# Block attention with a gated product: transposing q, k and the probabilities in two halves of 64 rows

## The chip, the core and the metric

The kernel runs on one core of a Trainium2 chip. The metric is the device time of one execution in microseconds (us), as the median of several executions. TensorE (PE in the rows) multiplies; its weight loads are listed apart as PEld. VectorE is DVE, ScalarE is ACT, GpSimd is POOL, and SyncE (SP) issues the DMAs.

## The reference

Attention over four batches of 8 heads, 768 positions and 64 columns a head, and a two-layer product over its result:

```python
k_sum = k.reshape(B, H, nb, 32, D).max(axis=3)        # 24 block maxima a head
v_sum = v.reshape(B, H, nb, 32, D).mean(axis=3)
scores_l = where(|i - j| < 16, scale * q @ k.T, -1e9)  # a window of 31 keys
scores_s = scale * q @ k_sum.T + log(32)
a = softmax(concatenate([scores_l, scores_s]))         # + 1e-9 in the divisor
x = a @ concatenate([v, v_sum])                        # then heads side by side: 3072 x 512
h = x @ w_in                                           # 512 -> 2048
out = (h - tanh(h)) @ w_out                            # 2048 -> 512
```

All inputs and the output are float32.

## The kernel before

**Tiling.** The 3072 positions are cut into 8 units (u) of 384, two to a batch, and a unit into three tiles of 128 rows. A unit has four pairs (p) of heads, so there are 32 pairs in all. The 16 column groups (f) of the 2048-wide layer run 22 slots behind the attention (LAG), so that from about 45 us on the two products of an earlier unit and the attention of a later one share TensorE. Products go in two parts, a rounded high word and a rest, three matmuls for one; units 2 to 7 combine two units at a time with seven products in place of eight.

**One pair.** `prep` (L821) transposes q and, from unit 2 on, the four tiles of keys of the pair, so that head columns lie on partitions: a transpose is a TensorE matmul of a 128x128 block against the identity. It is one task, "turn": three blocks of q into PSUM bank pS1 and four of k into bank pX. Two copies bring them to SBUF: "q high" (384 columns) and "k high" (512 columns). In unit 1 only q is transposed there, since the keys of units 0 and 1 are transposed once, in unit 0. `score` (L890) multiplies in blocks of 64x64, four of them side by side in the array, into banks pS0 and pS1. `softmax` (L923) leaves the probabilities of three tiles, each 128 rows x 118 columns for each of two heads. `transpose_probs` (L960) transposes a tile's two blocks in a task "p turn" and copies the 256 columns to SBUF in a task "p out"; the main loop calls it for the tiles one by one, with banks pS0, pX, pS1 (L1344). Then `value` (L900) multiplies them with v in blocks 64 columns wide, two side by side, into bank pX; the value matmuls of a pair stand in one task with the score matmuls of the next pair.

**Order.** The tasks are not emitted in the order of the code. `Plan.schedule` (L167) starts from costs a task, runs a list scheduler over the five engines, and emits the instructions in the order that it finds; on every engine they then run in that order, each waiting on semaphores for what it needs. Among ready tasks the one with the highest `level` goes first. The level is the longest chain of costs to the end, plus numbers from two tables: BIAS by task and KB by kind and phase. A third table (SL) says when a task goes to its second or third engine. A task on TensorE may leave a delay to the next product (LEAVES, L120); scores, values and the small transposes of sums are named there, "turn" and "p turn" are not. Where PE would idle in the first 100 us, matmuls of the identity fill in (`keep_warm`).

All instructions are recorded by a helper, so their line in the profile is L76; the tile names tell them apart. pS is pS0 or pS1, pX the third attention bank, pH the first product, pY0 to pY2 the second. In the profile a plain float32 matmul appears as two instructions, so `value` and `score` show 24 for 12 matmuls; a transpose shows as one.

Of the kernel before, what the change touches and what calls it, by code (L numbers as in the profile page):

```python
# [10 lines left out]
F32 = mybir.dt.float32  # L11
# [24 lines left out]
PROBS, PROBT = 3, 3  # L36
# [7 lines left out]

TOPS = {j: [(0, n)] for n, j in enumerate(PREP)}
SUMS = {1: [(0, 0), (0, 1)], 9: [(0, 2), (0, 3)]}

# [4 lines left out]
KB = {('chunk load', 0): 434.7, ('chunk max', 0): 88.2, ('chunk max', 1): -2.7, ('chunk sum', 0): -220.5, ('chunk sum', 1): -359.7, ('const', 0): -85, ('const', 1): -136.2, ('const', 2): -292.2, ('exp', 0): -33.6, ('g', 0): 13.2, ('g high', 0): -241.1, ('g low', 0): -310.4, ('in first', 0): -71.1, ('in first', 1): -182.2, ('inverse', 0): 28.8, ('join', 0): -293.9, ('join', 1): -75.7, ('k first', 0): -518.8, ('k first', 1): 106.5, ('k first', 2): 448.9, ('k high', 0): -153.3, ('k high', 1): -35.8, ('k keep', 0): 101, ('k keep', 1): -596.6, ('k keep', 2): -249.5, ('k load', 1): -310.2, ('k load', 2): -1.6, ('k move', 0): 111.7, ('k move', 1): -80.4, ('k move', 2): -200.1, ('key turn', 0): -255.8, ('key turn', 1): 120.7, ('key turn', 2): -1.5, ('mean out', 0): -253.8, ('mean out', 1): -79.7, ('mean put', 0): 93.1, ('mean put', 1): -73.6, ('mean put', 2): -2.8, ('mean turn', 1): 1.3, ('mean turn', 2): 20.1, ('min', 0): -0.6, ('normal', 0): 1.9, ('out first', 0): -357.5, ('out first', 1): -259.5, ('p out', 0): -27.4, ('p turn', 0): -1, ('part', 0): 89.2, ('part', 1): 385.1, ('q high', 0): -508.8, ('q load', 0): -35.5, ('q load', 1): 1.5, ('s high', 0): -41.2, ('s high', 1): 1.8, ('s high', 2): -462.5, ('s load', 0): -243.6, ('s load', 1): 1.6, ('s low', 0): 24.9, ('s low', 2): 102.6, ('s mix', 0): -358.8, ('s mix', 2): -480, ('s store', 0): -187, ('s store', 1): 0.7, ('s store', 2): -123.9, ('s whole', 0): 102.7, ('s whole', 1): -1.9, ('s whole', 2): 130.5, ('scores', 0): 1.4, ('seen', 0): 90.1, ('seen', 1): -77, ('seen', 2): -428.9, ('seen max', 0): -210.6, ('seen max', 1): 358.7, ('seen max', 2): 451.2, ('seen turn', 0): -0.7, ('seen turn', 1): 422.3, ('seen turn', 2): -9.1, ('series', 0): -201.9, ('square', 0): -65.5, ('sum', 0): 2.4, ('sum', 1): 419.6, ('sum', 2): -916.3, ('sum guard', 0): 59.1, ('tanh', 0): -2.1, ('top high', 0): 522.9, ('top high', 1): -162.7, ('top max', 0): 10.2, ('top max', 1): 238.5, ('top max', 2): -133.8, ('top pre', 0): -43.1, ('top pre', 1): 183.6, ('top pre', 2): -330.8, ('top put', 0): 0.1, ('top put', 1): -866.6, ('top put', 2): -26.1, ('top turn', 1): -172.1, ('top turn', 2): -472.6, ('turn', 0): 50.1, ('turn', 1): 211.7, ('v load', 1): -28.3, ('values', 1): -139.4, ('w high part 2', 0): -476.2, ('w high part 2', 1): 18.5, ('w high part 2', 2): -45.7, ('w load', 2): 227.6, ('w low', 2): 254.3, ('w low part 2', 0): -652.5, ('w low part 2', 1): -319, ('w low part 2', 2): -478.7, ('w scale', 2): -271.5, ('w shift', 1): 10.3, ('w shift', 2): -314.7, ('w sign', 0): -86.7, ('w sign', 2): -126.7, ('x high', 0): 646, ('x high', 1): -12, ('x low', 0): 282.9, ('x low', 2): -2, ('x mix', 0): 644.6, ('x mix', 1): 18, ('x whole', 0): -1.1, ('x whole', 1): -240.3, ('y out', 0): 157.1, ('y store', 0): -402.7}

HALF = {'const': (12, 12), 'k load': (33, 52), 'q load': (12, 24), 'top pre': (16, 16), 'v load': (44, 82), 'top turn': (8, 8), 'top max': (8, 8), 'q turn': (6, 15), 'q high': (12, 30), 'k turn': (6, 15), 'k high': (6, 15), 'top put': (7, 15), 'scores': (6, 14), 'sum': (8, 8), 'min': (30, 84), 'exp': (30, 84), 'sum out': (8, 8), 'sum guard': (5, 26), 'inverse': (5, 26), 'normal': (30, 84), 'p turn': (15, 42), 'p out': (15, 41), 'mean turn': (2, 4), 'mean out': (2, 4), 'mean put': (6, 14), 'values': (4, 4), 'x whole': (4, 9), 'w load': (13, 32), 'w scale': (12, 32), 'w shift': (12, 32), 'w low': (11, 32), 'w sign': (11, 32), 'w high part 2': (11, 32), 'w low part 2': (7, 32), 'in': (5, 33), 'square': (5, 33), 'tanh': (5, 32), 'series': (5, 32), 'g': (4, 32), 's store': (5, 48), 'out': (7, 96), 'x high': (0, 10), 'x low': (0, 10), 'y out': (0, 6), 'y store': (0, 6), 'g high': (0, 16), 'g low': (0, 16), 's whole': (0, 16), 's mix': (0, 32), 's high': (0, 16), 's low': (0, 16), 'chunk load': (0, 10), 'chunk max': (0, 4), 'chunk sum': (0, 4), 's load': (0, 3), 'x mix': (0, 1), 'top high': (0, 0), 'part': (0, 0), 'join': (0, 0), 'seen': (0, 0), 'seen turn': (0, 0), 'seen max': (0, 0), 'w high part': (3, 26), 'w low part': (3, 26), 'w sign 1': (4, 12), 'w sign 2': (4, 12), 'top low': (1, 2), 'cube': (2, 18), 'big': (2, 17), 'direct': (2, 17), 'pick': (2, 17), 'q low': (0, 2), 'q again': (0, 2), 'k low': (0, 2), 'k again': (0, 2)}


# [254 lines left out]
def program(  # L311
# [509 lines left out]
    def prep(u, p, tags):  # L821
# [4 lines left out]
        def transposes(ps, raw, n):  # L826
# [5 lines left out]
            for i in range(n):  # L832
                tensor.transpose(at(ps)[:, P * i:P * (i + 1)], raw[:, i, hs].rearrange("p a d -> p (a d)"), ident)
# [583 lines left out]
```

## Time and profile before

| What | Value |
|---|---|
| runs of the program | median 685.99 us (685.26 to 686.47, 3 runs) |
| span of the profiled execution | 682.6 us; no other time of this execution is given, and the median of the runs lies 3.4 us above the span |
| PE busy | 659.1 us, 97%, 4885 instructions |
| ACT busy | 491.2 us, 72% |
| DVE busy | 417.4 us, 61% |
| POOL busy | 206.8 us, 30% |
| granted clock of TensorE | 0.996 of full speed |
| DMA | 121.05 MB, 59.6% of 16 engines |

Busy time of PE counts an instruction from its start to its modelled end; matmuls overlap, so the mean of one (ns) is longer than the distance between two starts. How much of PE a kind of instruction takes is therefore read from the starts in the timeline. The number after a bar in the groups is the idle time of that engine before such instructions, with what ended it.

### The profile page before, as it was taken

The numbers are of one execution on the slowest core, as the hardware profiler recorded it, in microseconds if no ns is written. First come the engines' busy times: TensorE is split into PE (matmuls) and PEld (weight loads), VectorE is DVE, ScalarE is ACT, GpSimd is POOL, SyncE is SP. The second block draws the span as 40 slices with busy tenths as digits, with TensorE's granted clock in tenths as the row PEclk, the third lists the DMA queues.
The fourth block names the chain that finished last, engine by engine and source line by source line (L and its number), as shares of the span: only waits on it lengthen the run. The fifth ranks groups of instructions, "written<-read, shape, count | busy, mean of one in ns | idle before, by whom it ended". The sixth has DMA issues, their size and how long they took to land.

```text
span 682.6 us, 14370 instructions
## 1 busy us (share of the span) xinstructions
PE 659.1 (97%) x4885; PEld 549.1 (80%) x4885; DVE 417.4 (61%) x1183; ACT 491.2 (72%) x1445; POOL 206.8 (30%) x336
## 2 busy tenths in 40 slices
PE   7899999899999989999999999999999999999995
PEld 6665555478888877999888889899889889999884
DVE  3889988868897476555584574445576443323551
ACT  4888576778787787768984786766679946555882
POOL 2012222325355545312375642321124110000230
PEclk9999999999999998999999999999999999999999
DMA  8899999853766864785576456758435214453101
GB/s 242 218 260 286 292 291 271 275 156 136 214 190 192 269 186 135 192 220 172 133 233 187 119 139 211 221 156 213 141 116 158 105 62 147 161 170 123 48 1 52
DMA packets 145151, 121.05 MB, mean 177 GB/s; under 512 B 85036, under 2 KB 110892, under 8 KB 145068
## 3 DMA queue, kind: packets, MB, share of 16 engines
q1 hardware_dynamic: 145068, 120.03, 59.6%
q8 instruction: 41, 0.67, 0.4%
q14 instruction: 42, 0.34, 0.2%
HBM read 94.57 MB, written 23.07 MB: 172 GB/s over the span
## 4 chain that ended last, share of the span: by engine, by line
PE 85%; DMA 7%; DVE 3%; ACT 1%; SPq 1%; issue 1%; POOL 1%; ACTq 0%; POOLq 0%; DVEq 0%
PE pY L76 37%; PE pH L76 36%; PE pS L76 7%; PE pX L76 5%; DMA tmp<-in_k_dram 2%; SPq L76 1%; DMA wraw<-in_moe_w_in_dram 1%; DMA gu<-in_v_dram 1%; DMA wh<-in_k_dram 1%; DVE kacc L76 1%; DVE wraw L76 1%; DMA vw<-mean 1%; DMA rawk<-in_k_dram 1%; DMA out_dram<-tmp 1%; DMA scr<-wraw 1%
## 5 line engine op out<-in xcount | busy, mean ns | idle before, releaser
L76 PE MATMUL pY<-wf,gh 128*128 128x512 f32 x432 | 178.1, 439 | 2.9 <-POOL gh L76 2.9
L76 PE MATMUL pH<-wh,wraw 128*128 128x384 f32 x672 | 175.5, 342 | 0.1
L76 PE MATMUL pY<-wh,gh 128*128 128x512 f32 x336 | 137.0, 408 | 0.0
L76 PE MATMUL pY<-wh,gl 128*128 128x512 f32 x336 | 132.7, 395 | 0.0
L76 PEld LDWEIGHTS pH<-wh,wraw 128*128 128x128 f32 x672 | 121.4, 189 | 8.8 <-issue 1.2
L76 PE MATMUL pH<-wf,wraw 128*128 128x384 f32 x309 | 104.2, 337 | 0.0
L76 ACT ACTIVATE prob<-prob,stat 128x118 f32<-128x118 f32 x247 | 92.5, 384 | 12.7 <-DVE stat L76 11.3
L76 PEld LDWEIGHTS pY<-wf,gh 128*128 128x128 f32 x432 | 80.2, 189 | 25.4 <-issue 10.6
L76 PEld LDWEIGHTS pY<-wh,gl 128*128 128x128 f32 x336 | 63.2, 188 | 13.8
L76 POOL TENSOR_TENSOR gu<-gu,gt 128x384 f32<-128x384 f32 x31 | 33.7, 1087 | 128.8 <-ACT gu L76 127.7
L76 PEld LDWEIGHTS pY<-wh,gh 128*128 128x128 f32 x336 | 63.3, 188 | 10.9 <-issue 1.7
L76 ACT ACTIVATE gu<-gu 128x384 f32<-128x384 f32 x128 | 66.6, 521 | 1.8
L76 PE MATMUL pH<-o,wf 128*128 128x384 f32 x188 | 65.1, 442 | 2.0 <-ACT o L76 1.7
L76 PEld LDWEIGHTS pH<-wf,wraw 128*128 128x128 f32 x309 | 58.1, 188 | 0.0
L76 ACT ACTIVATE gu<-pH 128x384 f32<-128x384 f32 x65 | 31.7, 488 | 36.5 <-PE pH L76 33.5
L76 DVE CUSTOM_DVE_ANT_0 prob<-pS,mask 128x118 f32<-128x118 f32 x180 | 40.1, 275 | 28.8 <-PE pS L76 28.8
L76 PEld LDWEIGHTS pH<-o,wf 128*128 128x128 f32 x188 | 34.8, 189 | 19.7 <-issue 2.9
L76 ACT ACTIVATE gv<-pH 128x384 f32<-128x384 f32 x60 | 29.0, 484 | 27.0 <-PE pH L76 26.8
L76 DVE TENSOR_TENSOR gl<-gu,gh 128x384 fp32r<-128x384 f32 x43 | 27.0, 628 | 32.6 <-ACT gh L76 31.8
L76 POOL COPY k<-th 64x72 f32<-64x72 f32 (+1 forms) x45 | 12.7, 282 | 107.9 <-PE pS L76 86.3
L76 DVE TENSOR_TENSOR gu<-gu,gt 128x384 f32<-128x384 f32 x39 | 23.3, 596 | 35.9 <-ACT gu L76 35.8
L76 POOL TENSOR_TENSOR gl<-gu,gh 128x384 fp32r<-128x384 f32 x27 | 29.2, 1081 | 50.8 <-ACT gh L76 28.9
(211 smaller groups left out, 1242.5 us busy)
## 6 DMA issues: line engine op xcount, KB each, us to landing
wraw<-scr SPq DMA_DIRECT2D x75, 512.0 KB
wraw<-in_moe_w_in_dram SPq DMA_DIRECT2D x16, 512.0 KB
wraw<-in_moe_w_out_dram SPq DMA_DIRECT2D x16, 512.0 KB
scr<-wraw SPq DMA_DIRECT2D x16, 512.0 KB
rawq<-in_q_dram SPq DMA_DIRECT2D x42, 128.0 KB
out_dram<-tmp SPq DMA_DIRECT2D x21, 256.0 KB
wraw<-scr SPq DMA_DIRECT2D x21, 256.0 KB
scr<-wh SPq DMA_DIRECT2D x16, 256.0 KB
```

The costliest lines, as they stand in the source:

```text
L76: return lambda *args, **kwargs: self._tc.keep_in_program_order(op(*args, **kwargs))
```

## The change

In units 1 to 7 every 128-row block is transposed as two blocks of 64 rows: rows 0 to 63 with one half of the array's rows into one bank, rows 64 to 127 with the other half into a second bank. A half has the same 128 (or 118) columns as weights, and 64 columns of identity stream through instead of 128. q and k go into pS1 and pX together, half by half; the copies are split by halves too: two of 192 columns for q, two of 256 for k. The probabilities of a pair go, all three tiles, into pS0 and pX, and two copies of 384 columns replace three of 256. A tile's "p turn" is still a task of its own, but both copies wait for all three. Unit 0 keeps its old form. The order is planned anew: the level of a task is now minus a number from one table (TURNS_AT, 66 kinds, 3715 numbers) and no longer holds a chain of costs, BIAS or KB; SL and HALF are other numbers.

```diff
-PROBS, PROBT = 3, 3
+PROBS = 3
+TURN = 0.07
...
-BIAS = {('const', 0): -83.6, ('const', 1): -193.5, ('const', 2): -92.9, ...
+TURNS_AT = {'const': [199.57, 216.39, 42.37, 211.24, 201.89, 329.78, ...
...
-            t.level = max([n.level + (lag if data else 0.0) for n, data in t.next], default=0.0) + BIAS.get(t.name, 0.0) + KB.get((t.kind, phase(t)), 0.0)
+        for t in tasks:
+            at = TURNS_AT.get(t.kind, [0.0])
+            t.level = -at[min(t.name[1], len(at) - 1)]
...
+    def turn_half(out, x, half):
+        rows = slice(64 * half, 64 * half + 64)
+        tensor.transpose(out, x[rows], ident[rows, rows])
...
+        n = NT + 4 if u > 1 else NT
+        def turns():
             for i in range(n):
-                tensor.transpose(at(ps)[:, P * i:P * (i + 1)], raw[:, i, hs].rearrange("p a d -> p (a d)"), ident)
+                for half in range(2):
+                    x = rawq[:, i, hs] if i < NT else rawk[:, i - NT, hs]
+                    turn_half(at(ps[half])[:, 64 * i:64 * i + 64], x.rearrange("p a d -> p (a d)"), half)
+        do("turn", PE, TURN * n, turns, r=[*RAWQ, *(RAWK if u > 1 else []), IDENT], w=[(x, 0) for x in ps])
...
+        for half in range(2):
+            t = ps[half]
+            either("q high", {ACT: 0.28, DVE: 0.29}, lambda e, t=t, half=half: copy(e, at(qf)[:, 0].rearrange("p (i f r) -> p i f r", i=NT, f=2)[:, :, half], ...
+            if u > 1:
+                either("k high", {ACT: 0.32, DVE: 0.36}, lambda e, t=t, half=half: copy(e, k_runs(half), ...
...
+    def turn_probs(u, p, tags):
+        ps = [bank(("t", u, p, half), tag) for half, tag in enumerate(tags)]
+        pt = buf(("pt", u, p), "probT", [P, NT, 2, 2, 64])
+        def go(i):
+            for a in range(2):
+                for half in range(2):
+                    c = 64 * (2 * i + a)
+                    turn_half(at(ps[half])[:N2, c:c + 64], at(("pr", u, p, i))[:, a], half)
+        for i in range(NT):
+            do("p turn", PE, 2 * TURN, lambda i=i: go(i), r=[...], w=[(t, i) for t in ps])
+        for half, t in enumerate(ps):
+            either("p out", {ACT: 0.4, DVE: 0.47}, ..., r=[(t, i) for i in range(NT)], w=[(pt, half)])
...
-            for i, tag in enumerate((tags[2], tags[0], tags[1]) if early else (tags[0], tags[2], tags[1])):
-                transpose_probs(u, p, (i,), (tag,))
+            if early:
+                for i, tag in enumerate((tags[2], tags[0], tags[1])):
+                    transpose_probs(u, p, (i,), (tag,))
+            else:
+                turn_probs(u, p, (tags[0], tags[2]))
```

Three places in the order show it. The first is PE in unit 5. Before, between two pairs there stands (pS_4709 is bank pS0, pS_68 is pS1, rows with `wraw` or `gh` and `gl` are products of an earlier unit):

```order
L76 MATMUL pS_4709<-ident,prob 118x128 x2
L76 MATMUL pS_68<-ident,rawq 128x128 x3
L76 MATMUL pX<-ident,rawk 128x128 x4
L76 MATMUL pH<-q_3027,wraw 128x384 x3
L76 MATMUL pH<-wh_3277,wraw 128x384 x2
L76 MATMUL pH<-wf_3284,wraw 128x384
L76 MATMUL pH<-wh_3444,wraw 128x384 x2
L76 MATMUL pH<-wf_3460,wraw 128x384
L76 MATMUL pH<-wh_3624,wraw 128x384 x2
L76 MATMUL pH<-wf_3642,wraw 128x384
L76 MATMUL pX<-ident,prob 118x128 x2
L76 MATMUL pS_68<-ident,prob 118x128 x2
```

The transposes stand between products in two places, with the full array throughout. In the changed kernel, on PE between the same two pairs, two of the three tiles of probabilities (pS_4934 is pS0) stand together between products:

```order
L76 MATMUL pY_4774<-wh_978,gl 128x512
L76 MATMUL pS_4934<-ident,prob 118x64
L76 MATMUL pX<-ident,prob 118x64
L76 MATMUL pS_4934<-ident,prob 118x64
L76 MATMUL pX<-ident,prob 118x64
L76 MATMUL pS_4934<-ident,prob 118x64
L76 MATMUL pX<-ident,prob 118x64
L76 MATMUL pS_4934<-ident,prob 118x64
L76 MATMUL pX<-ident,prob 118x64
L76 MATMUL pH<-q_3073,wraw 128x384 x3
```

The halves alternate between the two banks, and the third tile comes some forty rows later, alone, after a transpose of block maxima (kacc):

```order
L76 MATMUL pS_68<-ident,kacc 128x96
L76 MATMUL pS_4934<-ident,prob 118x64
L76 MATMUL pX<-ident,prob 118x64
L76 MATMUL pS_4934<-ident,prob 118x64
L76 MATMUL pX<-ident,prob 118x64
L76 MATMUL pY_4863<-wh_1068,gh 128x512
```

So one pair has two stretches of halves for its probabilities, and a third for q and k, each with products ahead and behind it. The second place is PE at the end of unit 3. The changed kernel has this ahead of the values of the unit's last pair (pS_3676 is pS0; vacc is a sum of v, transposed by four small matmuls):

```order
L76 MATMUL pY_3268<-wh_814,gl 128x512
L76 MATMUL pS_3676<-ident,prob 118x64
L76 MATMUL pX<-ident,prob 118x64
L76 MATMUL pS_3676<-ident,prob 118x64
L76 MATMUL pX<-ident,prob 118x64
L76 MATMUL pS_68<-vacc,ident 24x64 x4
L76 MATMUL pX<-probT,vw 64x64 x12
```

Between the last half and the values that read its copy there is only the transpose of a sum. The third place is ACT: the copies of q and k of the changed kernel (q_164, k_82 are their SBUF tiles), between the exponentials and normalisations of a pair:

```order
L76 ACTIVATE prob,stat<-prob,stat 128x118 x3
L76 ACTIVATE q_164<-pX 128x3x64
L76 ACTIVATE q_164<-pS_68 128x3x64
L76 ACTIVATE k_82<-pX 128x4x64
L76 ACTIVATE prob<-prob,stat 128x118
L76 ACTIVATE k_82<-pS_68 128x4x64
```

Four copies stand where two did, each with half the columns.

## Rows read from the trace of the kernel before

**Rows 1.** The page: span, busy time of two engines, the chain by engine

```profile
span 682.6 us, 14370 instructions
...
PE 659.1 (97%) x4885; PEld 549.1 (80%) x4885; DVE 417.4 (61%) x1183; ACT 491.2 (72%) x1445; POOL 206.8 (30%) x336
...
PE 85%; DMA 7%; DVE 3%; ACT 1%; SPq 1%; issue 1%; POOL 1%; ACTq 0%; POOLq 0%; DVEq 0%
```

**Rows 2.** Waits of PE: us in total, times, longest; first and last of 14

```profile
PE pS L76 <- POOL ident L76: 4.3, 1, 4.3
...
PE pY L76 <- ACT probT L76: 0.2, 1, 0.2
```

**Rows 3.** Groups of PE by form: busy us, mean ns of one | idle before

```profile
L76 PE MATMUL pS<-ident,prob 128*118 128x128 f32 x120 | 21.3, 276 | 0.0
L76 PE MATMUL pX<-ident,rawk 128*128 128x128 f32 x96 | 14.6, 273 | 2.1 <-DMA rawk<-in_k_dram 2.1
L76 PE MATMUL pS<-ident,rawq 128*128 128x128 f32 x84 | 13.7, 272 | 0.0
L76 PE MATMUL pX<-ident,prob 128*118 128x128 f32 x60 | 11.5, 274 | 0.0
```

**Rows 4.** Timeline of PE, two tiles of probabilities transposed: start us, us, instructions

```profile
299.51 0.34 PE L76 MATMUL pH<-wf,wraw 128*128 128x384 f32 x1
299.68 0.38 PE L76 MATMUL pS<-ident,prob 128*118 128x128 f32 x2
299.90 0.38 PE L76 MATMUL pX<-ident,prob 128*118 128x128 f32 x2
300.04 0.60 PE L76 MATMUL pH<-wh,wraw 128*128 128x384 f32 x2
300.47 0.35 PE L76 MATMUL pH<-wf,wraw 128*128 128x384 f32 x1
```

**Rows 5.** Timeline of PE, values and scores between products

```profile
309.37 0.51 PE L76 MATMUL pH<-wh,wraw 128*128 128x384 f32 x2
309.71 0.34 PE L76 MATMUL pH<-wf,wraw 128*128 128x384 f32 x1
309.98 0.92 PE L76 MATMUL pX<-probT,vw 118*64 118x64 f32 x24
310.83 0.84 PE L76 MATMUL pS<-k,q 64*64 64x118 f32 x24
311.60 0.62 PE L76 MATMUL pH<-wh,wraw 128*128 128x384 f32 x2
```

**Rows 6.** The same values, timeline cut at 310.14 and at 310.61

```profile
309.98 0.34 PE L76 MATMUL pX<-probT,vw 118*64 118x64 f32 x4
...
309.98 0.80 PE L76 MATMUL pX<-probT,vw 118*64 118x64 f32 x20
```

**Rows 7.** Timeline of PE, the last pair's values, alone between products

```profile
508.72 0.92 PE L76 MATMUL pX<-probT,vw 118*64 118x64 f32 x24
509.57 0.62 PE L76 MATMUL pH<-wh,wraw 128*128 128x384 f32 x2
510.03 0.34 PE L76 MATMUL pH<-wf,wraw 128*128 128x384 f32 x1
```

**Rows 8.** Groups of weight loads by form: busy us, mean ns of one

```profile
L76 PEld LDWEIGHTS pX<-probT,vw 118*64 118x64 f32 x696 | 22.9, 137 | 11.8 <-issue 7.1 <-ACT probT L76 2.7 <-ACT gt L76 0.6
...
L76 PEld LDWEIGHTS pS<-ident,rawq 128*128 128x128 f32 x84 | 10.7, 141 | 3.6 <-issue 0.7 <-DVE stat L76 0.6 <-DVE tmp L76 0.2
```

**Rows 9.** Groups of ACT by form: the copies of p, q and k

```profile
L76 ACT ACTIVATE probT<-pS 118x256 f32<-118x256 f32 x48 | 18.0, 382 | 5.5 <-PE pS L76 5.3
...
L76 ACT ACTIVATE q<-pS 128x384 f32<-128x384 f32 x28 | 13.5, 482 | 1.5 <-PE pS L76 1.4
...
L76 ACT ACTIVATE k<-pX 128x512 f32<-128x512 f32 x14 | 8.3, 592 | 0.4 <-PE pX L76 0.4
```

More of the change, by code (lines that the diff above doesn't have):

```diff
@@ L177, in schedule @@
             t.count = len(t.after) + len(t.order)
-        for t in reversed(tasks):
-            e, cost = next(iter(t.costs.items()))
-            lag = cost + self.SEEN[e]
-            t.level = max([n.level + (lag if data else 0.0) for n, data in t.next], default=0.0) + BIAS.get(t.name, 0.0) + KB.get((t.kind, phase(t)), 0.0)
+        for t in tasks:
+            at = TURNS_AT.get(t.kind, [0.0])
+            t.level = -at[min(t.name[1], len(at) - 1)]
         engines = (PE, DVE, ACT, POOL, SP)
@@ L822, in prep @@
         hs = slice(2 * (p % PG), 2 * (p % PG) + 2)
-        pq, pk = bank(("pq", u, p), tags[0]), bank(("pk", u, p), tags[1]) if u > 1 else None
         qf, kf = ("qf", qk_of(u, p)), ("kf", qk_of(u, p))
+        if u:
+            prep_halves(u, p, hs, qf, kf, [bank(("pq", u, p, half), tag) for half, tag in enumerate(tags)])
+            return
+        pq = bank(("pq", u, p), tags[0])
         def transposes(ps, raw, n):
-            if in_runs(u):
-                for t in range(n):
-                    for a in range(2):
-                        tensor.matmul(at(ps)[D * a:D * (a + 1), :P * n].rearrange("p (r t) -> p t r", t=n)[:, t], by_runs(raw, n)[:, hs.start + a, t], ident, start=True, stop=True)
-                return
-            for i in range(n):
-                tensor.transpose(at(ps)[:, P * i:P * (i + 1)], raw[:, i, hs].rearrange("p a d -> p (a d)"), ident)
@@ L835, in turns @@
-        def turns():
-            transposes(pq, rawq, NT)
-            if u > 1:
-                transposes(pk, rawk, 4)
-        do("turn", PE, 0.8 if in_runs(u) else 0.763 if u > 1 else 0.327, turns, r=[*RAWQ, *(RAWK if u > 1 else []), IDENT], w=[(pq, 0), *([(pk, 0)] if u > 1 else [])])
-        either("q high", {ACT: 0.42, DVE: 0.5}, lambda e: copy(e, at(qf)[:, 0], at(pq)[:, :U], -1.0 / math.sqrt(D)), r=[(pq, 0)], w=[(qf, 0)])
+            for t in range(n):
+                for a in range(2):
+                    tensor.matmul(at(ps)[D * a:D * (a + 1), :P * n].rearrange("p (r t) -> p t r", t=n)[:, t], by_runs(raw, n)[:, hs.start + a, t], ident, start=True, stop=True)
@@ new lines, in prep, with prep_halves, k_runs @@
+        do("turn", PE, 0.8, lambda: transposes(pq, rawq, NT), r=[*RAWQ, IDENT], w=[(pq, 0)])
+        either("q high", {ACT: 0.42, DVE: 0.5}, lambda e: copy(e, at(qf)[:, 0], at(pq)[:, :U], -1.0 / math.sqrt(D)), r=[(pq, 0)], w=[(qf, 0)])
+    def turn_half(out, x, half):
+        rows = slice(64 * half, 64 * half + 64)
+        tensor.transpose(out, x[rows], ident[rows, rows])
+    def prep_halves(u, p, hs, qf, kf, ps):
+        n = NT + 4 if u > 1 else NT
+        def turns():
+            for i in range(n):
+                for half in range(2):
+                    x = rawq[:, i, hs] if i < NT else rawk[:, i - NT, hs]
+                    turn_half(at(ps[half])[:, 64 * i:64 * i + 64], x.rearrange("p a d -> p (a d)"), half)
+        do("turn", PE, TURN * n, turns, r=[*RAWQ, *(RAWK if u > 1 else []), IDENT], w=[(x, 0) for x in ps])
+        def k_runs(half):
+            x = at(kf)
+            return bass.AP(tensor=x.tensor, offset=x.offset + 64 * half, ap=[list(x.ap[0]), [KS, 4], [1, 64]])
@@ L844, in runs @@
             return bass.AP(tensor=x.tensor, offset=x.offset, ap=[list(x.ap[0]), [KS, 4], [1, P]])
[L845 to L848 removed]
+        for half in range(2):
+            t = ps[half]
+            either("q high", {ACT: 0.28, DVE: 0.29}, lambda e, t=t, half=half: copy(e, at(qf)[:, 0].rearrange("p (i f r) -> p i f r", i=NT, f=2)[:, :, half], at(t)[:, :64 * NT].rearrange("p (i r) -> p i r", i=NT), -1.0 / math.sqrt(D)), r=[(t, 0)], w=[(qf, half)])
+            if u > 1:
+                either("k high", {ACT: 0.32, DVE: 0.36}, lambda e, t=t, half=half: copy(e, k_runs(half), at(t)[:, 64 * NT:64 * (NT + 4)].rearrange("p (i r) -> p i r", i=4)), r=[(t, 0)], w=[(kf, 4 * half)])
+        if u == 1:
+            either("k move", {ACT: 0.49, DVE: 0.4, POOL: 1.2}, lambda e: copy(e, runs(), at(("kept", p)).rearrange("p (r c) -> p r c", r=4)), r=[(("kept", p), 0), (("kept", p), 1)], w=[(kf, 0), (kf, 4)])
     def all_keys(p, tag):
@@ L884, in score_keys @@
         n = qk_of(u, p)
-        return [(("qf", n), 0)] + [(("kf", n), x) for x in (0, "sums0", "sums1", *((1, "zero") if u == 0 else ()))]
+        return [(("qf", n), 0), *([(("qf", n), 1)] if u else [])] + [(("kf", n), x) for x in (0, "sums0", "sums1", *((1, "zero") if u == 0 else (4,)))]
     def score_of(u, p, i, a):
@@ L904, in value @@
                     c = P * i + 64 * half
-                    tensor.matmul(at(("px", u, p))[64 * a:64 * a + 64, c:c + 64], vw_of(u, p // PG, i)[:N2, half, 2 * (p % PG) + a, :], at(("pt", u, p, i))[:N2, a, half, :], start=True, stop=True)
+                    tensor.matmul(at(("px", u, p))[64 * a:64 * a + 64, c:c + 64], vw_of(u, p // PG, i)[:N2, half, 2 * (p % PG) + a, :], at(("pt", u, p))[:N2, i, a, half, :], start=True, stop=True)
     def value_keys(u, p):
-        return [(("pt", u, p, i), 0) for i in range(NT)] + [key for i in range(NT) for half in range(2) for key in vw_keys(i, half, second(u, p // PG))]
+        return [(("pt", u, p), n) for n in (range(NT) if u == 0 else (0, 1))] + [key for i in range(NT) for half in range(2) for key in vw_keys(i, half, second(u, p // PG))]
     def scores_and_values(now, before, tags, px_tag):
@@ L962, in transpose_probs @@
         banks = sorted({t for t, _ in at_of.values()})
-        for i in tiles:
-            buf(("pt", u, p, i), "probT", [P, 2, 2, 64], F32, PROBT)
+        pt = ("pt", u, p)
+        if pt not in made_by:
+            buf(pt, "probT", [P, NT, 2, 2, 64])
         def go():
@@ L973, in transpose_probs @@
             t, c = at_of[i]
-            pt = ("pt", u, p, i)
-            either("p out", {ACT: 0.265, DVE: 0.335}, lambda e, t=t, c=c, pt=pt: copy(e, at(pt)[:N2], at(t)[:N2, c:c + 2 * P].rearrange("p (a f r) -> p a f r", a=2, f=2)), r=[(t, 0)], w=[(pt, 0)])
+            either("p out", {ACT: 0.265, DVE: 0.335}, lambda e, t=t, c=c, i=i: copy(e, at(pt)[:N2, i], at(t)[:N2, c:c + 2 * P].rearrange("p (a f r) -> p a f r", a=2, f=2)), r=[(t, 0)], w=[(pt, i)])
+    def turn_probs(u, p, tags):
+        ps = [bank(("t", u, p, half), tag) for half, tag in enumerate(tags)]
+        pt = buf(("pt", u, p), "probT", [P, NT, 2, 2, 64])
+        def go(i):
+            for a in range(2):
+                for half in range(2):
+                    c = 64 * (2 * i + a)
+                    turn_half(at(ps[half])[:N2, c:c + 64], at(("pr", u, p, i))[:, a], half)
+        for i in range(NT):
+            do("p turn", PE, 2 * TURN, lambda i=i: go(i), r=[*((("pr", u, p, i), a) for a in range(2)), IDENT], w=[(t, i) for t in ps])
+        for half, t in enumerate(ps):
+            either("p out", {ACT: 0.4, DVE: 0.47}, lambda e, t=t, half=half: copy(e, at(pt)[:N2, :, :, half].rearrange("p i a r -> p (i a) r"), at(t)[:N2, :64 * 2 * NT].rearrange("p (n r) -> p n r", n=2 * NT)), r=[(t, i) for i in range(NT)], w=[(pt, half)])
     def x_buf(n, u, c, dtype=F32R):
```

11 lines of the change are left out of this document (3 added, 8 removed).

## The prediction

> **What bounds the kernel now.** I read the page first, then the waits of TensorE, then its groups by form, then the timeline around single transposes. The page shows TensorE busy for 97% of the span and holding 85% of the chain that ended last, with ACT at 72% [rows 1]. The waits of TensorE come to 16.4 us over 14 rows, and the longest, 4.3 us, is the identity at the start, which no order avoids [rows 2]. So the kernel is one long queue of TensorE work with some 12 us of holes, and the change is worth what it does to the time that this queue needs. Copies, loads and the other engines count only where they make TensorE wait.
>
> The span of the profiled execution is 682.6 us [rows 1]; the median of the three runs is 685.99, 3.4 us more, which I take for what lies around the span. I add changes of the span to 685.99.
>
> **What the change removes.** The groups to be replaced are the transposes of q, k and probabilities [rows 3]. In units 1 to 7 there are 28 pairs with three blocks of q and six of probabilities, and 24 of them have four blocks of k: 84 + 168 + 96 = 348 blocks. The 24 blocks of probabilities of unit 0 stay. One block costs TensorE the distance between two starts: two blocks start at 299.68 and the next two at 299.90, so 0.11 us each [rows 4], 0.109 when the same run is read to the nanosecond. Around them nothing is lost. The last product ahead starts at 299.51 and the first block 0.17 later, which is the pace of products (two start at 309.37, the third at 309.71, 0.17 each [rows 5]). Behind them, four blocks and two products take from 299.68 to 300.47, 0.79 us [rows 4], and 4 x 0.109 + 2 x 0.17 is 0.78. So a full-array transpose among full-array products costs 0.109 us and no changeover. All 348 cost 37.9 us.
>
> **What it adds: the halves.** No row shows a transpose in 64 rows. The nearest is `value`: it also streams 64 columns and also has two matmuls side by side in two parts of the array. When the timeline is cut after 4 and after 20 of its instructions, the last of them ends 0.46 us apart (0.80 - 0.34), for 16 instructions or 8 side-by-side pairs: 0.0575 us a pair [rows 6]. That fits half of 0.109. That two halves of the rows do run side by side into two banks is what `score` shows: 24 instructions of 118 columns take 0.77 us (310.83 to 311.60), 0.032 each, where one after the other they would need about 0.1 each at the pace of a 128-column block [rows 5]. The weights don't shrink, a half still loads 128 columns; but that load takes 141 ns against 137 for a load of `value` [rows 8], and `value` keeps two such loads in flight at its pace. So I take 0.0575 us a block, 20.0 us for 348, a gain of 17.9. From the other side, if the two halves follow each other, a block costs 2 x 0.0545 = 0.109 again and the gain is nothing.
>
> **What it adds: the changeovers.** Each stretch of halves has full-array products before and behind it, and the trace shows what such a stretch pays. Going in: the last product starts at 309.71, the first value at 309.98, 0.27 us where 0.17 is the pace, 0.10 more [rows 5]. Inside: the values take 0.85 us from their first start to the scores' first (309.98 to 310.83), and 12 pairs at 0.0575 are 0.69, so 0.16 more [rows 5, 6]. Going out: two products after the lone values of the last pair take 0.46 us (509.57 to 510.03) where two take 0.34, 0.12 more [rows 5, 7]; and those values also take 0.85 us to the next start (508.72 to 509.57), so the 0.16 belongs to leaving the mode, whatever it is left for [rows 7]. Together 0.37 us a stretch (0.38 in rounded rows, 0.36 to the nanosecond).
>
> The Trainium skill warns of just this: "TensorEngine Tiling (Array Packing)", section "Tiling Modes", says that changing the tiling mode, not just the tile, drains the engine. The trace agrees, with 0.10 us at the way in and 0.28 at the way out.
>
> In the order of the changed kernel the halves stand in 72 stretches that nothing else of their shape touches: 24 of seven blocks and 4 of three for q and k; 14 of six, 12 of four and 18 of two for the probabilities, since a pair's tiles become ready at different times and the planner sends them singly. By size, new against old:
> - seven blocks, 0.37 + 0.40 = 0.77 against 0.76: +0.01 x 24 = 0.2 us
> - six: 0.71 against 0.65: +0.06 x 14 = 0.9
> - four: 0.60 against 0.44: +0.16 x 12 = 2.0
> - three: 0.54 against 0.33: +0.21 x 4 = 0.9
> - two: 0.49 against 0.22: +0.27 x 18 = 4.8
>
> The sum is +8.8 us (72 x 0.37 = 26.6 paid, 17.9 gained). The new order has 41 other stretches off the full array where before there are 44, -1.1 us, and two stretches of halves run straight into a small one, about -0.2. That leaves +7.5 us for TensorE. The price is bounded by 0 a stretch below (the gain of 17.9 stands alone) and by 0.38 above, the largest that any row shows.
>
> **The copies.** q took 482 ns, k 592, a tile of probabilities 382 [rows 9]. From 256 to 384 columns ACT adds 100 ns, 0.78 a column, so 192 columns are about 332 ns. A pair now has 2 x 332 for q (+182), 2 x 382 for k (+172), and 2 x 482 in place of 3 x 382 for probabilities (-182): +0.17 us a pair, under 5 us over 28 pairs on ACT and DVE together. ACT is idle for 28% of the span [rows 1], and in nearly all pairs products stand between a turn and its reader, so I count nothing. If that cover were gone, it would be those 5 us. What does change is the wait: both copies of a pair's probabilities now wait for the last half, where two of three tiles were copied earlier. Behind the last half I find less cover than the copy needs in one place, the end of unit 3: only a transpose of a sum stands between, and the values wait behind it on TensorE with all products queued after them. A last half and copy of about 0.48 us plus two hand-overs make about 1.1, the sum's transpose covers about 0.65; I add 0.5 us. The next lowest has six products, 1.0 us.
>
> **The new order.** It moves loads, copies and products everywhere. TensorE's sequence keeps its shape (scores, turn, probabilities, values, at about the same distances), so I expect its waits to be about the old ones: 12 us that could go at best, and as much that could come. I take 0, with 4 us either way. TensorE later than planned gives loads and copies more time, which speaks against new waits.
>
> Sum: 685.99 + 7.5 + 0.5 = 694.0 us.
>
> **Rivals.**
> 1. *The changeover is cheap for 64-row halves.* It is the way it comes out faster. For it: every price above is from a mode that also splits the columns; the halves keep all 128 columns. Against it: between values and scores the columns stay split alike and only the rows change, and the 0.16 is paid there too [rows 5, 6]. At no price: 686 - 17.9 + 0.5 = 669; at half price, 72 x 0.185 = 13.3, about 681. It decides from 0.25 us a stretch downwards, where 72 stretches cost the 17.9 they gain. Chance 0.20, two thirds of it near the half.
> 2. *The halves don't overlap.* Then 348 blocks cost 37.9 as before and the 26.6 for changeovers is all added: 686 + 26.6 - 1.3 + 0.5 = 712. For it: a half loads as many weight columns as a whole block. Against it: rows 6 and 8. Chance 0.07.
> 3. *The new order fills the holes.* If two thirds of the 12 us of waits go while the halves cost +8: 686, no change. Chance 0.10. Nothing in the rows speaks for it, but the order is planned afresh from end to end.
>
> The same page, section "Theoretical Speedup", gives up to 2x for a dimension of 64 or less; by that alone the transposes would take 19 us less, an estimate that comes out with rival 1.
>
> **Numbers.** My forecast, halves side by side with the changeover paid, has 0.63; its own range is 689 to 700. The range for 8 in 10 runs from 677, which takes in the half price and leaves out the free changeover (0.07), to 703, which leaves out rival 2 and a little more. A difference under 0.2% (1.4 us) could not be told from none here. Faster has rival 1 and half of rival 3, 0.25; same 0.07; slower the rest, 0.68.
>
> **What will show it.** In the changed profile: the distance between two starts of one bank's halves (0.0575 us if side by side, 0.11 if not); from the last product to the first half, 0.27 us or 0.17; two products behind a stretch, 0.46 us or 0.34. If these hold and the time is not above 690, the new order has removed waits, and the waits of TensorE must be well under 16 us. A wait of the values for probT at the end of unit 3 should be there. I am wrong if a stretch of two blocks takes 0.25 us or less from product to product, or if waits of TensorE grow by more than 8 us.

## The result and the profile after

The changed kernel takes 692.85 us (692.45 to 695.23, 4 runs) against 685.62 us (685.05 to 686.47, 4 runs) for the kernel before. The ratio is 1.0124, with an interval of 1.0083 to 1.0166: slower, by 5.7 to 11.4 us. The medians are 7.2 us apart, a ratio of 1.0105 by themselves, and the forecast was 694.0.

The profiled execution took 695.23 us, 2.4 more than the median, with a span of 693.5. So 1.7 us lie around the span. The 3.4 us that the prediction took for this was a comparison of one execution's span with the median of others.

The page of the changed kernel, its span, busy time and chain (compare [rows 1]):

```profile
span 693.5 us, 15036 instructions
...
PE 670.4 (97%) x5239; PEld 539.9 (78%) x5239; DVE 431.4 (62%) x1220; ACT 481.8 (69%) x1436; POOL 198.1 (29%) x332
...
PE 80%; DMA 8%; ACT 3%; DVE 3%; SPq 1%; issue 1%; POOL 1%; POOLq 0%; ACTq 0%; DVEq 0%
```

TensorE's instructions grew by 354: 348 blocks became two halves each, and the rest are fillers. PE is busy for 11.3 us more, and the span is 10.9 us longer, so that is the whole growth: TensorE is still the bound, at the same 97%. (The two profiled executions lie further apart than the medians do.) The waits of PE in the changed kernel (us in total, times, longest), the first four and the last of 17 rows:

```profile
PE pS L76 <- POOL ident L76: 2.8, 1, 2.8
PE pH L76 <- DMA rawq<-in_q_dram: 2.0, 1, 2.0
PE pH L76 <- DMA wraw<-scr: 1.9, 3, 1.2
PE pH L76 <- DMA gu<-in_k_dram: 1.4, 1, 1.4
...
PE pH L76 <- ACT o L76: 0.2, 1, 0.2
```

They sum to 15.5 us, against 16.4 [rows 2]. No new wait explains the loss; the time is in the queue of matmuls itself. The timeline of PE around a stretch of two blocks in the changed kernel (start us, us, instruction):

```profile
326.53 0.40 PE L76 MATMUL pY<-wf,gh 128*128 128x512 f32 x1
326.76 0.40 PE L76 MATMUL pY<-wh,gl 128*128 128x512 f32 x1
327.09 0.27 PE L76 MATMUL pS<-ident,prob 64*118 64x64 f32 x1
327.09 0.27 PE L76 MATMUL pX<-ident,prob 64*118 64x64 f32 x1
327.20 0.22 PE L76 MATMUL pS<-ident,prob 64*118 64x64 f32 x1
327.20 0.22 PE L76 MATMUL pX<-ident,prob 64*118 64x64 f32 x1
327.35 0.50 PE L76 MATMUL pY<-wh,gh 128*128 128x512 f32 x1
327.68 0.40 PE L76 MATMUL pY<-wf,gh 128*128 128x512 f32 x1
327.92 0.39 PE L76 MATMUL pY<-wh,gl 128*128 128x512 f32 x1
```

Read it by the starts. Products stand 0.23 us apart where nothing is between them (326.53 to 326.76, 327.68 to 327.92). The first halves start 0.33 after the last product, 0.10 late. Two halves start together, one in each bank, so they do run side by side. The second pair starts 0.11 after the first, the next product 0.15 after that, and the product behind that one again 0.33 later, 0.10 late. From 326.76 to 327.68 are 0.92 us; two products alone need 0.46, so the stretch costs 0.46 us. Two whole blocks cost 0.22 [rows 4].

The same view at a stretch of seven blocks of q and k:

```profile
410.76 0.34 PE L76 MATMUL pH<-wf,wraw 128*128 128x384 f32 x1
411.03 0.27 PE L76 MATMUL pS<-ident,rawq 64*128 64x64 f32 x1
411.03 0.27 PE L76 MATMUL pX<-ident,rawq 64*128 64x64 f32 x1
...
411.39 0.28 PE L76 MATMUL pX<-ident,rawk 64*128 64x64 f32 x2
411.46 0.22 PE L76 MATMUL pS<-ident,rawk 64*128 64x64 f32 x1
411.61 0.50 PE L76 MATMUL pY<-wh,gh 128*128 128x512 f32 x1
411.95 0.40 PE L76 MATMUL pY<-wf,gh 128*128 128x512 f32 x1
```

Going in takes 0.27 where 0.17 is the pace [rows 5], the halves 0.58, and the product behind starts its follower after 0.34 instead of 0.23: 0.10 + 0.58 + 0.11 = 0.79 us, against 0.76 for seven whole blocks. Only here do the halves nearly pay for the changeover.

The halves of each bank by form in the changed kernel, then their weight loads and ACT's copies (count | busy us, mean ns | idle before), which answer to [rows 3], [rows 8] and [rows 9]:

```profile
L76 PE MATMUL pS<-ident,prob 64*118 64x64 f32 x168 | 19.2, 232 | 1.4 <-ACT prob L76 1.1 <-POOL prob L76 0.3
L76 PE MATMUL pX<-ident,prob 64*118 64x64 f32 x168 | 19.0, 231 | 0.0
L76 PE MATMUL pS<-ident,rawq 64*128 64x64 f32 x84 | 11.3, 240 | 1.2 <-DVE stat L76 1.2
L76 PE MATMUL pS<-ident,rawk 64*128 64x64 f32 x96 | 10.5, 225 | 0.7 <-DMA rawk<-in_k_dram 0.7
```

```profile
L76 PEld LDWEIGHTS pS<-ident,rawq 64*128 64x128 f32 x84 | 7.4, 138 | 11.3 <-DVE stat L76 5.6 <-issue 3.5 <-DVE prob L76 0.8
```

```profile
L76 ACT ACTIVATE probT<-pX 118x384 f32<-118x384 f32 x24 | 11.7, 489 | 1.9 <-PE pX L76 1.7
L76 ACT ACTIVATE q<-pX 128x192 f32<-128x192 f32 x28 | 9.1, 325 | 0.7 <-PE pX L76 0.7
L76 ACT ACTIVATE k<-pX 128x256 f32<-128x256 f32 x17 | 6.5, 380 | 1.1 <-PE pX L76 1.0
```

A half is drawn with 225 to 240 ns, hardly less than a whole block's 272 to 276, while the pairs, from the second on, start 58 to 63 ns apart: the mean of one is a latency and would have misled. A half's weight load of 128 columns takes 138 ns, where a whole block's took 141 [rows 8].

### The profile page after: what moved, and what is told of

Its sections match the earlier page's. It is cut to its first block, busy times and chain, and to the rows that moved or that the text cites. A ratio compares the mean times of both kernels' runs of the same rounds, so it can differ in the third digit from the quotient of the medians.

```text
span 693.5 us, 15036 instructions
## 1 busy us (share of the span) xinstructions
PE 670.4 (97%) x5239; PEld 539.9 (78%) x5239; DVE 431.4 (62%) x1220; ACT 481.8 (69%) x1436; POOL 198.1 (29%) x332
## 4 chain that ended last, share of the span: by engine, by line
PE 80%; DMA 8%; ACT 3%; DVE 3%; SPq 1%; issue 1%; POOL 1%; POOLq 0%; ACTq 0%; DVEq 0%
PE pY L76 35%; PE pH L76 35%; PE pS L76 7%; PE pX L76 4%; DMA wraw<-scr 2%; SPq L76 1%; DMA wraw<-in_moe_w_out_dram 1%; DVE kacc L76 1%; DMA wraw<-in_moe_w_in_dram 1%; ACT prob L76 1%; POOL tmp L76 1%; DMA gu<-in_k_dram 1%; DMA rawq<-in_q_dram 1%; ACT wh L76 1%; DVE wf L76 1%
## 5 line engine op out<-in xcount | busy, mean ns | idle before, releaser
L76 ACT ACTIVATE prob<-prob,stat 128x118 f32<-128x118 f32 x238 | 89.5, 385 | 15.1 <-DVE stat L76 13.8
L76 ACT ACTIVATE gv<-pH 128x384 f32<-128x384 f32 x46 | 22.5, 489 | 28.1 <-PE pH L76 27.1
L76 POOL TENSOR_TENSOR prob<-prob,stat 128x118 f32<-128x118 f32 x63 | 29.6, 485 | 39.7 <-DVE stat L76 36.2
```

The lines of the kernel that those rows point to most:

```text
L76: return lambda *args, **kwargs: self._tc.keep_in_program_order(op(*args, **kwargs))
```

## The experiments

My theory: the halves lose because each stretch of them costs TensorE a changeover of 0.37 us, and most stretches are too short to earn it back. The rival for the loss is the new order. The rest asks whether the changeover is one and whether the halves overlap.

**full_blocks, qk_halves, p_halves: the order without the halves, and each kind of halves alone.** All three keep the changed kernel's tasks, planned order and number of copies, and turn whole blocks of 128 rows in some or all of the 348 places:

```diff
-                    turn_half(at(ps[half])[:, 64 * i:64 * i + 64], x.rearrange("p a d -> p (a d)"), half)
+                    if half == n0 // 2:
+                        tensor.transpose(at(ps[half])[:, c:c + P], x.rearrange("p a d -> p (a d)"), ident)
...
-                    turn_half(at(ps[half])[:N2, c:c + 64], at(("pr", u, p, i))[:, a], half)
+                tensor.transpose(at(ps[i // 2])[:N2, c:c + P], at(("pr", u, p, i))[:, a], ident)
```

full_blocks has both edits, qk_halves the second alone, p_halves the first alone.

> The changed kernel with whole blocks of 128 rows again in all 348 places, in the same order of instructions, tasks and copies on every engine; a bank now holds whole blocks (two of q and two of k, one and two in the other), so a copy takes whole blocks, not halves, with about as many columns. Changeover theory: the stretches of halves lose 8.0 us in the changed trace (18 of two blocks at +0.244, 12 of four at +0.142, 14 of six at +0.041, 24 of seven at +0.023, 4 of three at +0.206), so this runs 692.9 - 8.0 = 684.8 us, within 2 of it. If the new order is what costs: 692 to 693. If the copies by halves cost: between, since their number stays: also near 692.

> The changed kernel, same order, with halves for q and k alone and whole blocks for the probabilities. Changeover theory: only 24 x 0.023 + 4 x 0.206 = 1.4 us of the loss stays, so 684.8 + 1.4 = 186.2 above 500, that is 686.2 us. If halves cost by the block, whatever the stretch, 180 of 348 blocks stay and half the loss: 689.

> The changed kernel, same order, with halves for the probabilities alone and whole blocks for q and k. Changeover theory: 44 of the 72 stretches stay, the short ones, with 18 x 0.244 + 12 x 0.142 + 14 x 0.041 = 6.7 us: 691.5 us. If halves cost by the block: 689.

Measured, against 684.71 us for the kernel before:

| Kernel | us | ratio | interval |
|---|---|---|---|
| full_blocks | 687.22 | 1.0043 | 1.0022 to 1.0065 |
| qk_halves | 689.04 | 1.0062 | 1.0032 to 1.0092 |
| p_halves | 691.56 | 1.0100 | 1.0065 to 1.0135 |

The new order, with the copies split as in the change, costs 0.43%, 2.9 us (1.5 to 4.4): more than the nothing I counted, and well under the loss of the change. This run can't part the order from the split copies. Over full_blocks, the halves of q and k add 0.19% (1.3 us; expected 1.4) and those of the probabilities 0.57% (3.9 us; expected 6.7). So the probabilities lose most, as by stretches, and not q and k, as they would have by the count of blocks. The intervals of these differences are wide, some 3 us. The granted clock hides a part: over its runs its mean was 0.9930 in full_blocks, 0.9928 in qk_halves and 0.9947 in p_halves. 0.0017 of 690 us are 1.2 us of full speed, so at one clock the halves of the probabilities would cost about 5 us (an estimate).

**one_task: the six blocks of a pair in one stretch, planned anew.**

```diff
-        for i in range(NT):
-            do("p turn", PE, 2 * TURN, lambda i=i: go(i), ...)
+        do("p turn", PE, 2 * TURN * NT, lambda: [go(i) for i in range(NT)], ...)
+        plan.count["p turn"] += NT - 1
+        plan.tasks[-1].name = "p turn", plan.count["p turn"]
```

> The changed kernel with the six blocks of probabilities of a pair in one task, with the number of the third tile in the table, so that they always stand in one stretch; the order is planned again with the same table. Changeover theory: 28 stretches of six in place of 44, 28 x 0.041 + 1.4 = 2.5 us of loss in place of 8.0, so 692.9 - 5.5 = 687.4 us, plus what the new waits cost, since the first tile now waits for the third: 0 to 3 us. If the number of stretches doesn't matter: 692.9 or more.

Measured: 732.10 us, 1.0705 (1.0666 to 1.0743). Neither theory comes near it, and the run says nothing on stretches, since the order fell apart. Its waits of PE, the first two rows:

```profile
PE pH L76 <- DMA wraw<-scr: 18.7, 7, 13.0
PE pY L76 <- POOL gl L76: 4.8, 6, 2.8
```

They come to 48.4 us in all, and the mean granted clock of its runs was 0.977, where the kernel before had 0.9956. The numbers of TURNS_AT were made for three tasks a pair; with another list of tasks the same table seems to put products ahead of the loads that they need, as the first row suggests.

**together: the same, with the plan kept.** The six blocks are emitted with the third tile's task, and the first two tasks are empty. The planner doesn't always place the third tile's task last, so in this kernel some tiles are transposed before they are normalised, and then a second version of the program runs behind the first.

```diff
-            do("p turn", PE, 2 * TURN, lambda i=i: go(i), ...)
+            do("p turn", PE, 2 * TURN, (lambda: [go(i) for i in range(NT)]) if i == NT - 1 else (lambda: None), ...)
```

> The changed kernel with its plan untouched, but the transposes of a pair's first and second tile are emitted with those of the third, so that the six blocks always stand in one stretch; the copies waited for the third tile before, too, so nothing else moves. Changeover theory: 28 stretches of six (28 x 0.041 = 1.1 us) in place of 44 (6.7 us): 5.5 us less TensorE time, so about 5 us under the changed kernel and near 1.005 times the kernel before. If a half costs the same in whatever stretch it stands: as the changed kernel, 1.012.

Measured: 1436.07 us, 2.0994 (2.0917 to 2.1071). It is the time of two programs (TensorE shows 10653 instructions, about twice the 5239 of the changed kernel) and tells nothing of stretches.

**not_alternating: one row half first, then the other.** The same halves in the same stretches and the same number of changeovers, but within a task all blocks of rows 0 to 63 come ahead of those of rows 64 to 127:

```diff
-            for i in range(n):
-                for half in range(2):
+            for half in range(2):
+                for i in range(n):
...
-            for a in range(2):
-                for half in range(2):
+            for half in range(2):
+                for a in range(2):
```

> The changed kernel, same order, but within a task all blocks of rows 0 to 63 come first and those of rows 64 to 127 after them. If the two halves of the array really work side by side, q and k lose the overlap (690 ns from first to last start in place of 430, 24 times, and 231 in place of 177 four times: +6.5 us; the probabilities, two blocks a task, about +0.4): near 700 us, 1.022 times the kernel before. If the overlap matters little: as the changed kernel, 1.012.

Measured: 699.04 us, 1.0213 (1.0179 to 1.0248), 0.8 to 0.9% or 5.3 to 6.1 us above the changed kernel (1.0124, and 1.0136 in a run below). The timeline of its PE at a seven-block stretch:

```profile
412.98 0.34 PE L76 MATMUL pH<-wf,wraw 128*128 128x384 f32 x1
413.25 0.40 PE L76 MATMUL pS<-ident,rawq 64*128 64x64 f32 x3
413.49 0.22 PE L76 MATMUL pS<-ident,rawk 64*128 64x64 f32 x1
413.49 0.27 PE L76 MATMUL pX<-ident,rawq 64*128 64x64 f32 x1
...
413.73 0.41 PE L76 MATMUL pX<-ident,rawk 64*128 64x64 f32 x4
414.07 0.50 PE L76 MATMUL pY<-wh,gh 128*128 128x512 f32 x1
```

The stretch takes 0.82 us from the first half to the next product, where it took 0.58 with the halves alternating. So alternating halves do work side by side, and the gain a block is real. Even here some of it stays: the second bank's halves begin at 413.49, while the first bank's are still coming.

**before_half and before_full: one small stretch, and its control.** In the order of before, one more transpose is added behind each of the 28 turns of units 1 to 7, into columns that nothing reads: once a single half of 64 rows, once a whole block.

```diff
+            if u: tensor.transpose(at(pq)[:, U:U + 64], rawq[0:64, 0, hs].rearrange("p a d -> p (a d)"), ident[0:64, 0:64])
```

```diff
+            if u: tensor.transpose(at(pq)[:, U:U + P], rawq[:, 0, hs].rearrange("p a d -> p (a d)"), ident[:])
```

> The kernel before, order untouched, with one 64-row half block added behind each of the 28 turns of units 1 to 7, into free columns of the bank, read by nobody. Changeover theory: each adds a stretch of its own, 0.095 in, 0.15 and 0.108 out, 0.35 us: +9.8 us, 1.014. If the price belongs to the blocks, not to the change of the array's mode: 28 x 0.06 = 1.7 us, 1.0025.

> The control to the run with one half block added: one whole block of 128 rows added in the same 28 places, twice the columns of a half. Changeover theory: 28 x 0.109 = 3.1 us, 1.0045, less than the half block although it is twice the work.

Measured, against 685.28 us: the half 688.22 us, 1.0065 (1.0032 to 1.0098); the block 682.21 us, 0.9975 (0.9946 to 1.0004). The half costs 0.9%, 6.0 us, more than the block, which has twice its rows: 0.21 us a place, where 0.24 was expected. The timelines of PE at one such place, first with the half, then with the block:

```profile
315.40 0.60 PE L76 MATMUL pX<-ident,rawk 128*128 128x128 f32 x4
315.93 0.27 PE L76 MATMUL pS<-ident,rawq 64*128 64x64 f32 x1
316.13 0.49 PE L76 MATMUL pY<-wh,gh 128*128 128x512 f32 x1
316.46 0.39 PE L76 MATMUL pY<-wf,gh 128*128 128x512 f32 x1
316.69 0.40 PE L76 MATMUL pY<-wh,gl 128*128 128x512 f32 x1
```

```profile
311.40 0.60 PE L76 MATMUL pX<-ident,rawk 128*128 128x128 f32 x4
311.84 0.27 PE L76 MATMUL pS<-ident,rawq 128*128 128x128 f32 x1
311.86 0.47 PE L76 MATMUL pY<-wh,gh 128*128 128x512 f32 x1
312.18 0.39 PE L76 MATMUL pY<-wf,gh 128*128 128x512 f32 x1
312.41 0.40 PE L76 MATMUL pY<-wh,gl 128*128 128x512 f32 x1
```

From the first block of k to the second product it is 1.06 us with the half and 0.78 with the block. A change of mode for one half shows on the half (0.53 after the first of the four blocks, where 0.44 is their pace) and on the product behind it (0.20 after the half, 0.02 after the block). The second product starts 0.33 after the first behind the half, but 0.32 behind the block too, so this delay is no mark of the mode: only the two distances together, 0.53 and 0.34, tell what leaving it costs. This is a change in rows alone, all 128 columns stay in use, and with the 0.11 of the block it costs 0.32 us by the times and 0.39 by these lines, about the 0.37 that the prediction took from modes that also split columns.

By the ratios both runs lie some 5 us under what was expected of them by themselves, and the added block even seems to be free. In its profile the half does add the time: PE is busy for 668.7 us, 9.6 more than before, where 9.8 was expected; with the block it is busy for 660.3. Their waits of PE are 10.5 us (half) and 11.5 us (block), where the kernel before showed 16.4 in its profile. That would fit, but these are single executions, and the kernel before itself ranged from 677.37 to 687.51 us beside them. Why is not settled; only the difference between the two is used.

**together_2 and after_again: fewer stretches in the same order.** The changed kernel's plan is left as it is, and the blocks of a pair are emitted where the last of its three tiles stands, so that the probabilities have 28 stretches of six in place of 44.

```diff
+        came = []
+        def last(i):
+            came.append(i)
+            if len(came) == NT:
+                for n in came:
+                    go(n)
...
-            do("p turn", PE, 2 * TURN, lambda i=i: go(i), ...)
+            do("p turn", PE, 2 * TURN, lambda i=i: last(i), ...)
```

> The changed kernel with its plan untouched, but all six blocks of a pair's probabilities are emitted where the last of its three tiles stands in the plan, whichever that is; the copies waited for the last one before, too. Changeover theory: 28 stretches of six blocks (28 x 0.041 = 1.1 us) and the 28 of q and k (1.4 us) stay, 2.5 us of 8.0, so 5.5 us less TensorE time: 4 to 5.5 us under the changed kernel on the same chip, about 1.005 times the kernel before, which the same order with whole blocks ran at 1.0043. If the number of stretches doesn't matter: as the changed kernel.

> The changed kernel once more, beside the run with the probabilities in one stretch on the same chip: 1.0124 times the kernel before, as first measured, within 0.3%.

Measured, against 685.48 us: together_2 689.86 us, 1.0073 (1.0045 to 1.0102); after_again 694.31 us, 1.0136 (1.0091 to 1.0182). The same halves in 16 stretches fewer take 4.5 us less (expected 4 to 5.5), 0.28 us for each stretch saved, where the price of a changeover is 0.35. This is the count of stretches by itself: as many halves, as many copies, the same order around them, and the same mean granted clock (0.992). None of the kernels beats the kernel before beyond doubt.

## Why the prediction was right, step by step

**The pace of a pair: right.** Predicted 0.0575 us; measured 0.058 (probabilities) and 0.063 (q and k), read to the nanosecond from the starts in one bank from the second pair on. Rival 2 falls by these starts and by not_alternating.

**The changeover: right.** Predicted 0.37 us a stretch. Of the two-block stretch above, 0.463 us read to the nanosecond, two pairs at 0.058 are 0.116, which leaves 0.35. It lies where values showed it [rows 5 to 7]: 0.10 going in, the rest at the second pair, at the product behind and at the one after it. The split was a little off: the second pair, 0.05 late, belongs to the way in, so that costs 0.15 us and the way out 0.20, where the prediction had 0.10 and 0.28. Rival 1, a cheap changeover for halves that keep all columns, falls by before_half against before_full.

**The sum over the stretches: nearly right in the trace, less in the time.** Read to the nanosecond, the stretches of the changed kernel cost more than whole blocks by 0.023 us (seven blocks), 0.041 (six), 0.142 (four), 0.206 (three) and 0.244 (two). Times 24, 14, 12, 4 and 18 that is 8.0 us, against 8.8 predicted. The ratios give 0.8 to 0.9% over full_blocks, 5.5 to 6.4 us. Their intervals don't exclude 8.0. Where the traces of after_again and full_blocks are laid beside each other by the share of product columns started, the difference grows by 5.7 us between 28% and 68% of them (270 to 520 us), where TensorE hardly waits and the stretches there come to 4.7. Before, part of it may be covered by waits for loads: between 24% and 28% (235 to 270 us) the stretches come to 0.6 us at most, and there the changed kernel, p_halves and qk_halves gain 1.0, 2.7 and 2.8 us on full_blocks in their traces, while after_again loses 1.1. The windows of before and of full_blocks (one row each) and of the changed kernel (two), by stretch, length, busy us and count of PE, PEld, DVE, ACT and POOL, granted clock, DMA share and GB/s:

```profile
200.00:300.00 100.00, 95.72 (x784) 84.05 (x779) 63.48 (x196) 76.10 (x239) 47.78 (x88) 0.98 0.69 197
```

```profile
200.00:300.00 100.00, 93.34 (x752) 80.27 (x751) 62.56 (x207) 71.70 (x233) 43.59 (x83) 0.97 0.66 187
```

```profile
200.00:300.00 100.00, 93.83 (x868) 76.83 (x866) 63.75 (x203) 72.38 (x233) 45.94 (x83) 0.98 0.66 188
300.00:520.00 220.00, 217.94 (x1857) 183.57 (x1856) 126.95 (x417) 156.56 (x491) 72.47 (x137) 1.00 0.60 173
```

From 200 to 300 us TensorE is busy for only 93% in full_blocks and 94% in the changed kernel, so there a longer stretch can take the place of a wait; from 300 to 520 us it is busy for 99% in the changed kernel, and there is no such room. That this is where the missing 2 us went is argued, not shown: each trace is one execution.

**The new order: the term that was mis-sized.** I counted -1.1 us for three fewer other stretches and otherwise nothing, 4 us either way; full_blocks shows +2.9 (1.5 to 4.4). It lies within the bounds, on the other side. The three were a miscount: in the traces 43 other stretches stand in the kernel before and 42 in the changed one, worth 0.4 us at most. Part of why the total came out close is that this error and the smaller effect of the stretches cancel. By the share of product columns, full_blocks is 3.0 us ahead of before at 16% of them and 1.5 behind at 28%; between, at 210 to 266 us, its TensorE waits for rewritten weights. 2.9 of these 4.5 us fall between 24% and 28%. The longest row of full_blocks's waits of PE:

```profile
PE pH L76 <- DMA wraw<-scr: 3.1, 2, 2.6
```

Yet the sum of its waits is 15.0 us, under the 16.4 of before, so waits alone don't make the 2.9. The granted clock makes a part of it. In the trace of full_blocks it falls to 1.2 GHz, half of full speed, at 256 us, behind waits of TensorE of 0.7 and 0.8 us and at the start of the longest, and stays there to 263; in that of before it is there from 258 to 261, behind a wait of 2.1 us. Over the runs of both kernels the mean granted clock is 0.9930 in full_blocks and 0.9956 in before, by which 1.8 of the 2.9 us would be lost clock (an estimate: 0.70% and 0.44% of the spans). Which part of the order makes the rest, and the waits ahead of the falls, was not tried. Rival 3, an order that fills the holes, falls by full_blocks.

**The wait at the end of unit 3: there, smaller.** Predicted 0.5 us. The timeline of PE in the changed kernel at this place, with the idle time in brackets:

```profile
271.18 0.22 PE L76 MATMUL pX<-ident,prob 64*118 64x64 f32 x1
271.33 0.63 PE L76 MATMUL pS<-vacc,ident 96*24 96x64 f32 x8
272.17 0.92 PE L76 MATMUL pX<-probT,vw 118*64 118x64 f32 x24 [0.22 <-DVE probT L76]
```

The sum's transpose covers all but 0.22 us of the last copy.

**The copies: right.** q, k and probabilities take 325, 380 and 489 ns on ACT, where 332, 382 and 482 were worked out from [rows 9], and they show nowhere in TensorE's waits beyond that one.

## What to carry to other kernels

Before a matmul is split so that its parts run side by side in the array, count how often the array changes between split and whole in the order that will run, and price a change from the starts in the timeline, from the matmul before to the second one behind. Hold these starts against the same ones around whole blocks, since a product can come late behind those, too. Here a change costs about as much as three whole transposes, the gain a block is not quite half of one, and a stretch of seven blocks still lost 0.02 us. An order made from a table of times belongs to the tasks that it was made for: one_task lost 7% to it.

## What the runs showed of the hardware

- A single half-array transpose among whole ones costs more than the whole block it could replace: in this case the half made the kernel 6.0 us slower than the block did, in 28 places.
- The cost of leaving the half mode can't be read from one product: behind a half the first product starts 0.20 us after it and the second 0.33 later, behind a whole block 0.02 and 0.32. The second is late against its pace of 0.23 in both cases; the sum is 0.19 us longer behind the half.
- Two halves with 118 or 128 weight columns each keep a pace of 58 to 63 ns a pair, although a half's weight load is drawn with 138 ns: loads of several halves are in flight at once.
- Time goes with the granted clock of TensorE: of two runs of the kernel before, one took 677.37 us at a mean clock of 0.998 and one 687.51 us at 0.992. In the traces of before and full_blocks the clock falls to 1.2 GHz at 258 and 256 us, where TensorE waits for loads and for another engine.
